# New written-out orders for two attention cores, two FFT convolutions and a front, with whole-tile and half-column forms of three PE steps

## The chip, the core and the metric

The kernel runs on one core of one Trainium2 chip, in one launch. The metric is the device time of an execution in microseconds (us), lower is better. The engines: TensorE (PE; its weight loads are listed as PEld), VectorE (DVE), ScalarE (ACT), GpSimd (POOL), and SyncE (SP), which here only issues DMAs.

## The reference

Two kinds of layers alternate, A, B, A, B, on a 2048 x 512 sequence in bf16. Both second layers use the same weights as the first ones.

```python
# A: dilated sliding-window attention, 32 heads of 16, window W=8, dilation 2
qkv = x @ wqkv                                   # (2048, 3*512)
idx = pos[:, None] - arange(8) * 2               # masked where negative
logits = einsum("bhsd,bhswd->bhsw", q, k[:, :, idx]) * 16**-0.5
attn = softmax(where(mask, logits, -1e9))
out = einsum("bhsw,bhswd->bhsd", attn, v[:, :, idx]) @ wo
# B: S4 layer, a causal convolution by FFT over 4096 points
K = einsum("dn,dnl,dn->dl", Cc, exp(dt*A*l), dt*Bc).real      # 512 x 2048
y = irfft(rfft(u, 4096) * rfft(K, 4096))[:2048] + u * Dskip
# the whole
x = x + A(layernorm(x)); x = x + B(layernorm(x))
x = x + A(layernorm(x)); x = x + B(layernorm(x))
```

## The kernel before, in words

The residual x_sb lies in SBUF with the sequence on 128 partitions x 16 rows (rows a = 0 to 15) and 512 features free. The execution has these stages, one after the other on the span of the profile: the filter K of layer B with the first front (layer norm, transposes, first projections), 0 to 110 us; the first attention core ("core 0"), 110 to 193; the first convolution ("conv 0") with the transform of the filter, 193 to 250; the second front, 250 to 275; "core 1", 275 to 365; "conv 1", 365 to 411; then the rest of the output's store.

**Who sets the order.** Nothing is scheduled: `tc.manual_schedule` keeps the instructions of DVE, ACT, PE and SP in the order of the program, and the program's order is written out in strings. CORE0 and CORE1 have one letter for each step of attention; ORDER0, ORDERF and ORDER1 have one token for each tile of the convolutions and the front. An engine takes its instructions in that order and waits at the first that isn't ready.

**A core** works on four blocks q of four rows. Letters: `q`, `v` project queries and values on PE (L215, L388) with a copy on ACT; `m` (mult, L332) multiplies queries with the eight shifted views of the keys on DVE into prod, two buffers; `l` (lsum, L340 to L344) sums each prod over the features of a head on PE into the logits L; `x` takes the maximum (mx, L404, DVE), `e`, `r`, `n` do exp, sums and normalisation (L416 to L438). A block below NCOL has its logits in columns (L340) and needs `T` (turn: transposes L444 on PE, a copy L446 on ACT); the others have them in rows (L344). `P` (pv_mult, L457, DVE) multiplies attention weights with eight shifted views of the values into pav, two buffers; `S` (pv_sum, L472, PE) transposes and sums pav in 64 half tiles of 64 partitions into po, copied by ACT to oT (L474); `O` (out_proj, L481, L483) projects and adds the residual. `a`, `b`, `d`, `t` are the layer norm of the result. In CORE0 the letters `A` to `H` copy eighths of the filter (k_part, L1379), turn about on ACT and DVE.

**A convolution** works on two halves g of the features. Tokens: `K`/`U` are f1 tiles of filter and signal (first FFT step, L769 on PE, evacuated from PSUM by evac, L758); `k`/`u` are f2 tiles (L776), u copied by ACT to ub (L835); `m` (u_mult, L819, L822) multiplies by the filter's transform on DVE; `y` (i1, L849) is the first inverse step, evacuated to z (L758); `z` (i2, L873 to L875) the second inverse step for four rows and one half g, which adds the residual, either on DVE while evacuating (L878) or by a matmul with the identity (L873) and a copy on ACT (L880). The letter at a token's end names the engine of the evacuation: A is ACT, D is DVE, B is half on each. In conv 1 the filter's transforms come from DRAM through a ring, kf_ring, whose loads SP issues. An i1 tile is 32 pairs of weight load and matmul on the two halves of the partitions:

```python
for tt, w, first in ((t1, C["Wp"], True), (t2, C["WpJ"], False)):
    for h in range(2):
        rows = slice(64 * h, 64 * h + 64)
        nc.tensor.matmul(p3[:, h, j, :], lhsT=tt[rows, dql, :], rhs=w[rows]..., start=first, stop=not first)
```

**The second front** (ORDERF) interleaves the last i2 tiles of conv 0 with layer norm (h, a, p, n), transposes (T) and the projections of keys and queries (P, E, Q) for core 1.

## Time and profile before

| what | value |
|---|---|
| runs | 413.06, 412.20, 412.77 us; median 412.77 |
| the profiled execution | 416.72 us; its span in the profile 414.9 us |
| instructions, bytes moved | 14876; 54.17 MB |
| mean granted clock of PE | 0.985 |
| DVE, L457 pav | 34 of 2.16 us on average, 72.9 us |
| DVE, L332 prod | 29 of 2.31 us, 66.3 us |
| ACT, L835 ub | 32 of 1.04 us, 32.1 us |
| PE, L472 po | 2048 matmuls, 35.9 us |

The span is the time from the first to the last instruction that the profiler recorded; what lies around it is 1.8 us here. A duration of a matmul in the profile is from its issue to its modelled end, and matmuls overlap, so the distance between the starts of two tiles tells more than their durations. "<-" names what ended a wait; "issue" is time in which nothing that the profile shows was waited for.

### The profile page before, as it was taken

What the parts mean: (1) busy time and instruction counts of PE and PEld (TensorE: products, weight loads), DVE (VectorE), ACT (ScalarE), POOL (GpSimd) and SP (SyncE); (2) the same over time, 40 slices, a digit from 0 to 9 for tenths busy, and PEclk for the clock granted to TensorE, in tenths of its full rate; (3) what the DMA queues carried; (4) which work ended last, traced back from release to release, by engine and by line L of the source; (5) the groups of instructions that cost most, each with busy time, mean ns of one, the idle gap of its engine ahead of it and who ended that gap; (6) DMA issues with size and microseconds to landing.
All of it is one profiled execution on the core that took longest, in us unless ns stands there. A gap on an engine that the chain in (4) does not pass through costs nothing.

```text
span 414.9 us, 14876 instructions
## 1 busy us (share of the span) xinstructions
PE 323.9 (78%) x6575; PEld 216.5 (52%) x6575; DVE 383.1 (92%) x500; ACT 327.9 (79%) x561; POOL 37.0 (9%) x48
## 2 busy tenths in 40 slices
PE   2000159899999977889997779999998889997785
PEld 2000126557533555656887668543445555576664
DVE  7999999999899999997998968979899999999965
ACT  5999999896456689997999988874666768889942
POOL 3000200000495000001300000000000020000000
PEclk9999999999999999999999999999999999999988
DMA  7930732122014845493244594830043046406406
GB/s 216 397 109 13 83 82 71 33 60 71 13 44 127 237 132 173 112 379 108 79 153 173 202 318 107 317 116 0 2 115 91 3 148 270 150 2 176 134 9 197
DMA packets 62322, 54.17 MB, mean 131 GB/s; under 512 B 33869, under 2 KB 50738, under 8 KB 60978
## 3 DMA queue, kind: packets, MB, share of 16 engines
q1 hardware_dynamic: 62250, 53.22, 41.7%
q8 instruction: 51, 0.84, 0.8%
q14 instruction: 13, 0.11, 0.1%
q10 hardware_dynamic: 8, 0.00, 0.0%
HBM read 30.15 MB, written 13.24 MB: 105 GB/s over the span
## 4 chain that ended last, share of the span: by engine, by line
PE 38%; DVE 20%; ACT 11%; issue 6%; DMA 6%; SPq 4%; DVEq 0%; ACTq 0%
PE pk L1195 5%; DVE prod L332 5%; PE pq L388 5%; DVE pav L457 4%; PE pp L1133 4%; DVE a1s L758 4%; PE po L472 3%; PE pq L483 3%; PE pp L272 3%; PE pq L215 3%; SPq L1300 2%; DMA w_sb<-w_dram 2%; PE L L340 2%; DMA kf_ring<-kf_dram 2%; DVE t L822 2%
## 5 line engine op out<-in xcount | busy, mean ns | idle before, releaser
L457 DVE TENSOR_TENSOR pav<-attn,v_ext 128x4096 bf16<-128x4096 bf16 (+1 forms) x34 | 72.9, 2155 | 0.4 <-PE pq L483 0.4
L332 DVE TENSOR_TENSOR prod<-qT,kT_ext 128x4096 bf16<-128x4096 bf16 x29 | 66.3, 2313 | 2.9 <-PE L L340 1.8
L472 PE MATMUL po<-ident,pav 64*128 64x64 bf16 x2048 | 35.9, 190 | 11.1 <-DVE pav L457 5.7
L472 PEld LDWEIGHTS <-pav 64*128 64x128 bf16 x2048 | 32.6, 95 | 22.1 <-DVE pav L457 12.3
L1123 PE MATMUL pt<-ident,x_blk 128*128 128x128 bf16 x64 | 6.3, 241 | 41.0 <-ACT x_blk L187 41.0
L1037 DVE TENSOR_TENSOR A_t<-A_t,pow_t 128x1024 bf16<-128x1024 bf16 (+4 forms) x46 | 38.1, 868 | 0.2
L776 PE MATMUL pb<-a1s,w_sb 128*128 128x64 bf16 x768 | 28.7, 196 | 6.9 <-ACT a1s L758 2.7
L483 PE MATMUL pq<-wop,oT 128*128 128x512 bf16 x128 | 33.7, 387 | 0.0
L835 ACT CAST ub<-pb 128x1024 bf16<-128x1024 f32 x32 | 32.1, 1038 | 1.8 <-ACT a1s L758 0.9
L388 PE MATMUL pq<-wv,xnT 128*128 128x512 bf16 x128 | 30.8, 380 | 0.3 <-ACT kgs L1203 0.3
L1133 PE MATMUL pp<-xnT,kT_ext 128*128 128x512 bf16 x96 | 26.2, 400 | 6.0 <-ACT qT L1138 3.1
L776 PEld LDWEIGHTS <-w_sb 128*128 128x128 bf16 x768 | 26.1, 100 | 9.3 <-issue 7.3
L758 DVE CAST a1s<-pb 128x1024 bf16<-128x1024 f32 x23 | 27.0, 1215 | 3.4 <-PE pb L769 3.4
L390 ACT CAST v_ext<-pq 128x512 bf16<-128x512 f32 x32 | 18.8, 587 | 14.3 <-PE pq L388 14.3
L1123 PEld LDWEIGHTS <-x_blk 128*128 128x128 bf16 x64 | 4.8, 108 | 43.4 <-ACT x_blk L187 42.0
L758 ACT CAST a1s<-pb 128x1024 bf16<-128x1024 f32 x25 | 24.9, 1036 | 2.2 <-PE pb L769 1.9
L474 ACT CAST oT<-po 128x512 bf16<-128x512 f32 x32 | 18.5, 578 | 8.1 <-PE po L472 7.8
L1195 PEld LDWEIGHTS <-A_t 128*64 128x64 bf16 (+1 forms) x512 | 21.8, 103 | 4.1 <-issue 0.6
L1195 PE MATMUL pk<-B_t,A_t 128*64 128x84 bf16 (+1 forms) x512 | 23.6, 201 | 0.0
L215 PE MATMUL pq<-xnT,kT_ext 128*128 128x512 bf16 x96 | 23.5, 379 | 0.0
L849 PEld LDWEIGHTS <-t 64*128 64x128 bf16 x1024 | 17.5, 97 | 11.4 <-issue 9.7
L849 PE MATMUL pb<-Wp,t 64*128 64x64 bf16 x512 | 19.5, 193 | 4.6 <-ACT ub L835 1.8
(240 smaller groups left out, 814.4 us busy)
## 6 DMA issues: line engine op xcount, KB each, us to landing
w_sb<-w_dram SPq DMA_DIRECT2D x8, 1024.0 KB, 7.1
w_dram<-xnT SPq DMA_DIRECT2D x1, 4096.0 KB
kf_ring<-kf_dram SPq DMA_DIRECT2D x13, 256.0 KB, 4.2
kf_ring<-kf_dram SPq DMA_DIRECT2D x26, 128.0 KB, 3.9
v_ext<-v_ext SPq DMA_DIRECT2D x4, 784.0 KB, 5.9
x_blk<-in_A_x_dram SPq DMA_DIRECT2D x4, 512.0 KB, 4.5
kT_ext<-in_A_wqkv_dram SPq DMA_DIRECT2D x4, 512.0 KB, 9.9
x_sb<-in_A_x_dram SPq DMA_DIRECT2D x4, 512.0 KB, 5.5
```

Source lines behind the costliest of these rows:

```text
L215: nc.tensor.matmul(pq[:], lhsT=self.wqk[:, dt, ft * P:(ft + 1) * P], rhs=self.xnT[:, dt, q * 512:(q + 1) * 512], start=(dt == 0), stop=(dt ...
L332: nc.vector.tensor_tensor(pr, self.qT[q][:, ft].unsqueeze(1).to_broadcast([P, W, 4, P]), kap, ALU.mult)
L388: nc.tensor.matmul(pp[:], lhsT=xnT[:, dt, a * P:(a + 1) * P], rhs=wv[:, dt, :], start=(dt == 0), stop=(dt == NDT - 1))
L457: nc.vector.tensor_tensor(pv[:, i], attn[:, n % 4].unsqueeze(2).to_broadcast([P, W, DH // parts, H]), vap, ALU.mult)
L472: nc.tensor.matmul(po[:, h, 0, i * nt + ft, :], lhsT=pvf[rows, i, w, ft * P:(ft + 1) * P], rhs=ident[rows, rows], start=(w == 0 and ft + i ...
L483: nc.tensor.matmul(pw[:], lhsT=oT[:, ftp, :], rhs=self.wo[:, ftp, :], start=False, stop=(ftp == NDT - 1))
L758: (self.nc.scalar.copy if eng == "act" else self.nc.vector.tensor_copy)(dst, src)
L776: nc.tensor.matmul(p2[:, j, :], lhsT=self.w2[:, ec * EC + j, :], rhs=a1s[:, ec * EC + j, :], start=True, stop=True)
L849: nc.tensor.matmul(p3[:, h, j, :], lhsT=tt[rows, dql, :], rhs=w[rows].rearrange("p m d -> p (m d)"), start=first, stop=not first)
L1037: return lambda: nc.vector.tensor_tensor(*args)
L1133: nc.tensor.matmul(pps[kind, b, ft][:], lhsT=la.wqk[:, dt, c:c + P], rhs=la.xnT[:, dt, b * 512:(b + 1) * 512], start=(dt == 0), stop=(dt = ...
L1195: nc.tensor.matmul(o, lhsT=lhs, rhs=Bt[:, ri, c * CH + ql].rearrange("p b g -> p (b g)"), start=(not half and j % 4 == 0 and ri == 0), sto ...
```

## The change

All of the order strings but the filter's (ORDERK) are new. Besides the order they change which engine evacuates which tile, and use new letters. `V` is a pv_sum that sums whole tiles of 128 partitions, 32 matmuls of 128 columns instead of 64 of 64 (one in core 0, five in core 1). `Y` is an i1 tile with whole weights, 16 matmuls of 128 columns instead of 32 of 64 (three in conv 0, two in conv 1); for it Wp and WpJ are stored once for each half of the partitions, with zeros in the other half. `w` and `v` are i2 tiles of half a g's columns, over eight rows with DVE's addition or over four rows with ACT's copy. In conv 1, w00, w01 stand for z00, z01, and v10, v11 for z10; z01 of conv 0 moves from ORDERF to the end of ORDER0. NCOL goes from 3 to 2 in both cores, so block 2's logits go into rows and its turn is gone. KROWS gives the last eighth of the filter's copy (`H`) to ACT instead of DVE. The unused tile "gap" of core 0 grows from 1024 to 1680 elements for each partition, and the tile of layer-norm statistics ln_bn is halved.

The number of PE matmuls goes from 6575 to 6513; DVE has two instructions fewer, ACT one copy more.

```diff
@@ -48,34 +48,35 @@
 zktkKkUEETkeUUktKTkkUkKTUUeKkkpkxpKUxkpUEUxUKkqUxUUUUpqoUkpoxKXUQxoUkpkKXZpxXxpxZZ
 """
 ORDER0 = """
-KD KA KA KD KA KA KD KA KD KA KD kA kA KD kA KD UA UD UA UD UA kD UA UD UA KD
-kA kD u kD kA u UA m KD m u u UD UA UA UA m UD u m KA UD u m u kA kD m kA UA
-kD u kA m kA kD u m u kA m m u u yD yA u m yA u m m m u u m m
+KD KD KA KA KA KD KA KA KD KA KD kA KD kA KD UA UA kD UA UA UD kA UD UA UA KD
+kA kD u kD kA u UA m KD u u m UA m UD UD UA UA u m KA u u m UD kA
+m u kD kA m kA kD kD UA kA u kA u m yA m u m yD yA u u m YA m m
+u u m m yA u m yA yA YD yD yA YD yA yA z01D yD yA
 """
 LATE0 = "a s t g r b m"
 ORDERF = """
-yA yA yA yA yA yA yD yA yA yA z01D yD yA yA z00A z10A z11A h01 h00 h10 a0 z12A
-p0 h11 z02A n0 a1 z03A h02 S T0 p1 E01D n1 E00A h12 a2 z13A P02 P01 h03 T1
-E10A Q00 E11D p2 P03 P00 n2 h13 P10 P12 a3 T2 E21D E20A p3 n3 P11 P13 P23 P21
-T3 E31D x1 E30A P20 P22
+yA z00A z10A h01 h00 h10 z11A a0 z12A h11 p0 S z02A n0 a1 z03A h02 p1 T0 E01D n1 h12 a2 E00A
+z13A P01 P02 T1 E11D E10A h03 Q00 p2 P00 n2 P03 h13 P10 P12 P11 T2 a3 E20A p3 E21D n3 P13 P23
+P20 P21 T3 E31D x1 E30A P22
 """
 ORDER1 = """
-UD UA UD UA UD UA UD UA UD UA UD u UD u u m UA u m UD UA m u m u m
-u m UA m u m u m u m u u yD yA u m yA m m u u u m yA m yA
-yA m yD yD yA yD yA yA yA yD z01D z03D yA yA z00D z02D z12D z11A z10D z13B
+UA UD UA UD UA UD UD UA UA UD UA u UD u u m u m m UA m u UD u m u
+UA m UA u u m m u m u m u yD m u yA yA m m u m u yA m u m
+yA yA yD YD yA YA yD z03D yD yA yA w000D yA yA w010D z02D v100A v110A z11A z12D z13B
 """
 
 CORE0 = """
-0mvvvvlmvvxlemqqlmqqlrmvvlnTmvvxlvemvlmvvlrmvvlnTqPxSePmqSOl1PrSO2Pm3qSOlPnT4SOPm56qSOl7P8ASOPmbBSO
-lPxdwCSeOPaaDSOPraaSOPnbSOPd9ESOPaaFGSOPaaHSOPbtStO
+vmvvv0lvmvqxleqqmlmvrlqmvvnTlmvvxlmevmlvvrlmvvlnTqPxSePS1qmOlPr4SO2PmqS3OlnP5SP67qmOSOlP8ASOPmPb
+BOSlCSwxdeOPaSaarPODVOPnbSOPd9SEOaaPaSOPGFaaPtOSHbSOt
 """
 CORE1 = """
-0m1l2ml3mqqlmqqvlmvvxlvemvvlmqqlrmqqvlnTmvvxlvemvvlmvvlrmvvlPnTqxSePmqSOlPrSOPmqSOlPnTSOPmqSOlPSO
-PmbSOlPxdwSeOPaaSOPraaSOPnbSOPdSOPaaSOPaaSOPbtStdaaaaO
+0m1l2ml3mvmqqqqlmlvmvvvxlqmvleqlrqmqlnTvmvvxlemvmvlvrvlmvvvlPnSTxqePSOmlqPrVOqOPmSPlnSOPOmqSlPVO
+PmbVOPlxdaVeOrPawSOPaaVOPnbSOPdSOPaSOPPaatSObStadaaaaO
 """
 ROWS0 = (0, 2, 1, 3, 4, 5, 6, 7, 8, 9, 10, 11, 12, 13, 14, 15)
 ROWS1 = (0, 2, 1, 3, 4, 5, 6, 7, 8, 9, 10, 11, 12, 13, 14, 15)
-NCOL = (3, 3)
+NCOL = (2, 2)
+KROWS = "ADADADAA"
 VROWS = (*range(0, 16, 2), *range(1, 16, 2))
 
 
@@ -366,7 +367,7 @@
                 self.load_wo(big)
             wk = c2.enter_context(tc.tile_pool(name=f"a{l}_wk", bufs=2, reuse_waits="tile"))
             if l == 0:
-                wk.tile([P, 1024], BF16, name="gap", bufs=1)
+                wk.tile([P, 1680], BF16, name="gap", bufs=1)
             self.prp = c2.enter_context(tc.tile_pool(name=f"a{l}_prod", bufs=2, reuse_waits="tile"))
             pavp = c2.enter_context(tc.tile_pool(name=f"a{l}_pav", bufs=2, reuse_waits="tile"))
             ps_q = c2.enter_context(tc.tile_pool(name=f"a{l}_ps_q", bufs=2, space=PSUM))
@@ -457,13 +458,23 @@
                     nc.vector.tensor_tensor(pv[:, i], attn[:, n % 4].unsqueeze(2).to_broadcast([P, W, DH // parts, H]), vap, ALU.mult)
                 pvs[n] = pv
 
-            def pv_sum(n):
+            def pv_sum(n, whole=False):
                 pv = pvs.pop(n)
                 parts = pv.shape[1]
                 pvf = pv[:].rearrange("p i w d h -> p i w (d h)")
                 po = ps_o.tile([P, 2, 2, NDT, 64], F32, name="po")
                 oT = wk.tile([P, NDT, P], BF16, name="oT")
                 nt = NDT // parts
+                if whole:
+                    pw = po[:, 0].rearrange("p b t q -> p (b t q)").rearrange("p (t q) -> p t q", t=NDT)
+                    for i in range(parts):
+                        for w in range(W):
+                            for ft in range(nt):
+                                nc.tensor.matmul(pw[:, i * nt + ft, :], lhsT=pvf[:, i, w, ft * P:(ft + 1) * P], rhs=ident[:],
+                                                 start=(w == 0 and ft + i == 0), stop=(w == W - 1), skip_group_check=True)
+                    nc.scalar.copy(oT[:], pw)
+                    oTs[n] = oT
+                    return
                 for i in range(parts):
                     for w in range(W):
                         for ft in range(nt):
@@ -533,17 +544,19 @@
                 m=calls(mult, *qft[nprod:]), l=calls(logit(lsum), *qft[nprod:]),
                 q=calls(q_proj, *qft[len(self.qT) * NDT:]), v=calls(v_proj, *((a,) for a in VROWS)),
                 x=calls(mx, *blocks), e=calls(sub_exp, *blocks), r=calls(recip, *blocks), n=calls(norm_p, *blocks), T=calls(turn, *blocks[:ncol]),
-                P=calls(pv_mult, *rows), S=calls(pv_sum, *rows), O=calls(out_proj, *rows[:15]), t=calls(x_stats, (12,), (13,)),
+                P=calls(pv_mult, *rows), O=calls(out_proj, *rows[:15]), t=calls(x_stats, (12,), (13,)),
                 b=calls(u_begin, (0, 4, "act", "pool"), (4, 8, "act", "act"), (8, 12, "act", "act")),
                 d=calls(u_end, (0,), (4,), (8,)),
                 a=calls(u_apply, *((a0, (a,)) for a0 in (0, 4) for a in range(a0, a0 + 4)), *((8, (a,), "act" if l and a < 10 else "dve") for a in range(8, 12))))
             ops = {key: iter(f) for key, f in ops.items()}
+            sums = iter(rows)
+            ops["S"], ops["V"] = (iter([lambda w=w: pv_sum(*next(sums), w)] * NA) for w in (False, True))
             for c in "".join(order.split()):
                 if c in ev:
                     ev[c]()
                 else:
                     next(ops[c])()
-            assert all(next(ops[c], None) is None for c in "mlqvxernPSOtb")
+            assert next(sums, None) is None and all(next(ops[c], None) is None for c in "mlqvxernPOtb")
             if l == 0:
                 out_proj(15)
                 return {"a": lambda: [u_end(8), u_apply(8, range(8, 12), "pool")], "s": lambda: x_stats(14), "t": lambda: x_stats(15),
@@ -662,9 +675,12 @@
             sine(ws[name][:], low16(wt[name][:].rearrange("p r a -> p (r a)")))
 
         def w_mask(name):
-            C[name] = cpool.tile([P, 32, 2], BF16, name=name)
-            nc.gpsimd.tensor_tensor(C[name][:], ws[name][:].unsqueeze(2).to_broadcast([P, 32, 2]),
-                                    dmask_m.unsqueeze(1).to_broadcast([P, 32, 2]), ALU.mult)
+            C[name] = cpool.tile([P, 2, 32, 2], BF16, name=name)
+            nc.gpsimd.memset(C[name][:], 0.0)
+            for h in range(2):
+                r = slice(64 * h, 64 * h + 64)
+                nc.gpsimd.tensor_tensor(C[name][r, h], ws[name][r].unsqueeze(2).to_broadcast([64, 32, 2]),
+                                        dmask_m[r].unsqueeze(1).to_broadcast([64, 32, 2]), ALU.mult)
 
         def w2_store():
             for s in range(4):
@@ -834,22 +850,25 @@
         ub = self.ub[g * NEC + ec] = self.wk.tile([P, DQG, EC], BF16, name="ub")
         nc.scalar.copy(ub[:], p2)
 
-    def i1(self, g, t, eng):
+    def i1(self, g, t, eng, whole=False):
         nc, C = self.nc, self.C
         if t == 0:
             self.S[g]["z"] = self.z0 if g == 0 else self.gpair("z", "t")[:, 0].rearrange("p (m c) -> p m c", m=2 * NA)
         z = self.S[g]["z"]
         t1, t2 = (self.S[g]["t"][:, i] for i in range(2))
-        p3 = self.ptile([P, 2, DQT, 64])
+        p3 = self.ptile([P, DQT, 2, 64] if whole else [P, 2, DQT, 64])
         for j in range(DQT):
             dql = t * DQT + j
             for tt, w, first in ((t1, C["Wp"], True), (t2, C["WpJ"], False)):
+                w = w[:].rearrange("p h m d -> p h (m d)")
+                if whole:
+                    nc.tensor.matmul(p3[:, j], lhsT=tt[:, dql, :], rhs=w, start=first, stop=not first)
+                    continue
                 for h in range(2):
                     rows = slice(64 * h, 64 * h + 64)
-                    nc.tensor.matmul(p3[:, h, j, :], lhsT=tt[rows, dql, :], rhs=w[rows].rearrange("p m d -> p (m d)"),
-                                     start=first, stop=not first)
+                    nc.tensor.matmul(p3[:, h, j, :], lhsT=tt[rows, dql, :], rhs=w[rows, h], start=first, stop=not first)
         self.evac(z[:, :, t * DQT * 4:(t + 1) * DQT * 4].rearrange("p m (j h d) -> p m j h d", h=2, d=2),
-                  p3[:].rearrange("p h j (m d) -> p m j h d", d=2), eng)
+                  p3[:].rearrange("p j h (m d) -> p m j h d" if whole else "p h j (m d) -> p m j h d", d=2), eng)
 
     def i2(self, g, t, eng):
 
@@ -878,6 +897,25 @@
             nc.vector.tensor_tensor(xr, p4[:], xr, ALU.add)
         else:
             nc.scalar.copy(x_sb[:, a0:a0 + n, dsl], p4[:])
+
+    def i2_cols(self, g, c, b, n, eng):
+
+        nc, x_sb, z = self.nc, self.x_sb, self.S[g]["z"]
+        w = DQG * 2
+        zs, a0 = slice(c * w, (c + 1) * w), b * n
+        xr = x_sb[:, a0:a0 + n, (2 * g + c) * w:(2 * g + c + 1) * w]
+        p4 = self.ptile([P, n, w])
+        add = eng == "dve"
+        for j in range(n):
+            a = a0 + j
+            if not add:
+                nc.tensor.matmul(p4[:, j, :], lhsT=self.ident[:], rhs=xr[:, j], start=True, stop=False)
+            nc.tensor.matmul(p4[:, j, :], lhsT=self.g2[:, 0, a, :], rhs=z[:, a, zs], start=add, stop=False)
+            nc.tensor.matmul(p4[:, j, :], lhsT=self.g2[:, 1, a, :], rhs=z[:, NA + a, zs], start=False, stop=True)
+        if add:
+            nc.vector.tensor_tensor(xr, p4[:], xr, ALU.add)
+        else:
+            nc.scalar.copy(xr, p4[:])
 
     def run(self, order, u, done=lambda g, t: None, k=None, late=(), more={}):
         late, cnt = list(late), self.cnt
@@ -895,6 +933,15 @@
                 self.i2(*ix, eng)
                 done(*ix)
                 continue
+            if op in "wv":
+                rows = 8 if op == "w" else 4
+                self.i2_cols(*ix, rows, eng)
+                for b in range(ix[2] * rows // 4, (ix[2] + 1) * rows // 4):
+                    half = cnt["w", ix[0], b] = cnt.get(("w", ix[0], b), 0) + 1
+                    if half == 2:
+                        done(ix[0], b)
+                continue
+            op = "y" if op == "Y" else op
             n = cnt[op] = cnt.get(op, -1) + 1
             g, t = divmod(n, 8)
             if op in src:
@@ -912,7 +959,7 @@
             elif op == "m":
                 self.u_mult(g, t)
             else:
-                self.i1(g, t, eng)
+                self.i1(g, t, eng, tok[0] == "Y")
 
     def swap_psum(self):
         self.c_ps.close()
@@ -1375,7 +1422,7 @@
         nc.vector.tensor_tensor(kr[0:1, 0, :], kr[0:1, 0, :], dsk[:, h * 256:(h + 1) * 256], ALU.add)
 
     def k_part(h, j):
-        cp = nc.scalar.copy if j % 2 == 0 else nc.vector.tensor_copy
+        cp = nc.scalar.copy if KROWS[h * 4 + j] == "A" else nc.vector.tensor_copy
         cp(kp[:, h * 64 + j * 16:h * 64 + (j + 1) * 16, :, :],
            krs[h][:, :, j * 64:(j + 1) * 64].rearrange("p a (q r) -> p q a r", r=4))
 
```

More of the change, by code (lines that the diff above doesn't have):

```diff
@@ L1336 @@
     lnst = dict(s1=cpool.tile([P, NA], F32, name="ln_s1"), s2=cpool.tile([P, NA], F32, name="ln_s2"),
-                bn=cpool.tile([P, NA, 2, 6], F32, name="ln_bn"), junk=cpool.tile([P, D], BF16, name="ln_junk"),
+                bn=cpool.tile([P, NA, 1, 6], F32, name="ln_bn"), junk=cpool.tile([P, D], BF16, name="ln_junk"),
                 mh=cpool.tile([P, 4], F32, name="ln_mh"))
```

## The prediction

> **What bounds the kernel now.** I read the page first, then the table by stage, then the chain that ended last, VectorE's (DVE's) own timeline, and the waits.
>
> The page's totals, and its row for the queue that brings instructions:
>
> ```profile
> PE 323.9 (78%) x6575; PEld 216.5 (52%) x6575; DVE 383.1 (92%) x500; ACT 327.9 (79%) x561; POOL 37.0 (9%) x48
> q8 instruction: 51, 0.84, 0.8%
> ```
>
> DVE is the bound on average, but a share of 92% leaves 31.8 us of the 414.9 in which it waits. TensorE (PE) has 6575 matmuls and as many weight loads, 13,150 instructions; 51 packets of instructions is one per 258 of them. In the packets' own rows each holds 16 KB, 256 instructions of 64 bytes, and almost all are PE's.
>
> The table by stage (columns: length, then busy time of PE, PEld, DVE, ACT, POOL; granted clock, DMA share, GB/s):
>
> ```profile
> 110.00:193.00 83.00, 73.17 (x1482) 41.17 (x1483) 78.19 (x61) 62.53 (x126) 20.82 (x17) 1.00 0.51 156
> 193.00:238.00 45.00, 39.16 (x1216) 35.16 (x1215) 43.10 (x58) 42.71 (x48) 6.05 (x8) 1.00 0.43 155
> 238.00:252.00 14.00, 10.92 (x360) 9.14 (x360) 8.92 (x16) 12.24 (x14) 0.35 (x1) 1.00 0.88 287
> 252.00:275.00 23.00, 22.90 (x180) 14.77 (x179) 19.75 (x69) 18.34 (x33) 0.00 (x0) 1.00 0.65 218
> 275.00:364.00 89.00, 83.47 (x1536) 44.96 (x1534) 85.22 (x71) 60.84 (x130) 2.89 (x1) 0.98 0.27 91
> 364.00:415.00 51.00, 38.20 (x1098) 33.35 (x1096) 41.62 (x40) 35.88 (x40) 0.00 (x0) 0.91 0.36 105
> ```
>
> These are core 0 (attention), convolution 0 up to its last u tile, its end, the second front, core 1, convolution 1 with the store. The cores are DVE's; convolution 0 is shared by DVE and ACT to within an evacuation; the front is PE's (22.90 of 23); the two ends of the convolutions belong to nobody, and there the time is to be had.
>
> The chain in the last 20 us, from where the last u_mult (L819) has ended:
>
> ```profile
> 394.86 0.39 issue
> 395.25 1.22 DVE xnT L758
> 396.51 0.38 PE pb L849 x14
> 396.89 1.46 issue
> 398.35 1.93 PE pb L849 x82
> ```
>
> PE stops in the middle of an i1 tile (L849), 14 matmuls into it, for 1.46 us, waiting for nothing that the profile shows. Counted in program order, that instruction is the first of a block of 256. The others fall on boundaries too: 390.35, 394.35, 398.35 are three in a row, 4.0 us apart, and 247.34 (a stop of 1.10 in the chain) is one in convolution 0. The fetch rows show why 4.0: a packet starts 1.5 to 1.7 us after PE has entered a block (392.05, 395.95) and the next block is entered 2.3 to 2.4 us after that. So a block that PE could run in less than 4.0 us still takes 4.0. A block of half-tile i1 is four tiles of 0.47 us (starts of L849 tiles, 394.61, 395.07, 395.54): 1.9 us of work. Its effect on DVE:
>
> ```profile
> 396.38 1.21 DVE L758 CAST z<-pb 128x1024 bf16<-128x1024 f32 x1
> 400.32 1.23 DVE L758 CAST z<-pb 128x1024 bf16<-128x1024 f32 x1 [2.74 <-PE pb L849]
> 402.14 2.35 DVE L878 TENSOR_TENSOR x_sb<-pb,x_sb 128x1024 bf16<-128x1024 f32 x2 [0.59 <-PE pb L875]
> ```
>
> After the gaps the clock halves: i2 matmuls are 0.21 us apart from 400.2 to 402.2 and 0.11 after that.
>
> Core 0's waits on DVE:
>
> ```profile
> DVE a1s L758 <- PE pb L769: 2.4, 1, 2.4
> DVE prod L332 <- PE L L340: 1.8, 1, 1.8
> DVE mx L404 <- PE L L322: 0.8, 1, 0.8
> ```
>
> **Basis.** The profiled execution took 416.72 us (span 414.9 and 1.8 around it), 3.95 above the median of the runs, 412.77. Differences are worked out on its rows and taken from the median unscaled (1% of 7 us is nothing). A change under 0.2%, 0.8 us, can't be told from none.
>
> **The change part by part.**
>
> *Convolution 1, up to the last u_mult.* One f1 tile goes from DVE to ACT: DVE has seven of 1.13 us back to back (8.01 for 7 at 365.76) where it had eight, and its u_mults follow without a gap in both. DVE is solid from 365.76 to 397.6, so −1.1. ACT gains 0.92 there and has slack (its idle in the tail alone is 8 us); two u tiles come so close to their mults that 0.3 may be lost. Filter loads (kf_ring, SP's queue) move with the mults that free their slots. Taken: −0.9.
>
> *Convolution 1, the end.* Call T0 the end of the last mult, 394.11 less a fraction in before; DVE's last operation ends at 410.96, T0+16.85. After: two of the sixteen i1 tiles are whole (16 matmuls of 128 columns, 32 instructions instead of 64). No row has that form; by streaming, 16×128 columns against 8×256 of an i2 tile (L874/875, 8×0.11) is 0.88 us. w000D, w010D are 16 matmuls of 128 columns, 0.88 as well; v100A, v110A 12 of them, 0.66; instead of three i2 tiles of 0.88. So PE gets 0.82 more to do, and 2×32 instructions less in i1. Laid on the new program order with the same offset: the block that straddles T0 holds 3 half tiles and 2 whole (3.2 us), the next 3.6 half tiles, z03 and 5 matmuls of w000 (2.85), the one behind it 5.2 us, the last 2.75. The straddling one is entered about T0−1.6 (last u copy ends T0−1.2, the f2 tile before it about T0−2.3, then 1.4 i1 tiles). By the rule of 4.0 the others are entered at T0+2.4, T0+6.4 and, unstopped, T0+11.6; PE ends at T0+14.4, the last evacuation of half a tile (0.59) at T0+15.0. DVE has 10.9 us of work there, which fits. Gain 1.85. If the clock halves again for 2 us, 1 us of it goes; if the blocks cost nothing, 1.7 more comes. Bounds 0 and −3.5; taken −1.9.
>
> The Trainium skill, "Runtime: NRT & Kernel Launch", section "Instruction fetch mechanics", says that the sequencer fetches the next 16 KiB (256 instructions) while it executes the current ones, and that crossing costs little, "mostly hidden". By that rule the stops above aren't the blocks', and the sum for this part would be about 0. The trace agrees on the 256 and not on the hiding: 1.46 us of stop at 396.89.
>
> *Convolution 0.* Evacuations: ACT one fewer in all (y 13→11, U 10→11; 0.95), DVE one more (1.13). ACT is the bound up to 249.85, where the front's first copy stands: 53.3 busy of 56.3, and 1.28 of its idle time is the stop at 247.34. But the order also moves work: in front of the last u, ACT has three more evacuations and DVE one fewer, which fills ACT's 2.3 us of idle time and delays the last u by 1 to 2.5. Behind it, ACT has 7 i1 tiles instead of 11 and PE 720 instructions instead of 912 (three whole tiles, two of them here). In blocks: the last f2 stands just ahead of a boundary, the next two blocks (2.5 and 3.3 us of work) take 4.0 each, then 2.1 tiles: the front's first tile begins 9.2 us behind the last f2, in before 13.05 (235.28 to 248.33). So −3.85 and +1 to +2.5: −1.35 to −2.85, and −2.2 by ACT's account (0.95+1.28). Taken −2.1. At 287 GB/s the block before 247.34 took 4.8 us instead of 4.0, so bounds 0 and −4. Three half-tile pairs becoming whole cost PE 1.2, behind evacuations.
>
> *Second front.* The same seven ACT-form i2 tiles of 12×0.109 us, transposes and projections; z01D moved ahead of it. PE-bound before and after: 0 (±0.5); it passes on what convolution 0 wins.
>
> *Core 0.* k_part H moves from DVE (0.41, L1379) to ACT (1.03); ACT loses one attn copy after turn (1.01, L446), since the third block's logits now go into rows. So ACT is even, DVE −0.4. Turn's 8 transposes (0.46) go, lsum gets 0.25 to 0.4 longer, four times (row form 0.80 to 0.95, column form 0.55): PE +0.9, hidden behind 78.19 us of DVE. mx of the last block stands later behind mults: its 0.8 goes, and if the logits come late it returns as up to 1.8 (the prod wait). At the handover one f1 tile of the filter stands ahead of row 15's pv_sum on PE; DVE's first a1s can start at once and the second waits as in before: 1.0 of the 2.42. The copy of H may delay oT by 0.5. Sum −0.4−0.8−1.0+0.3 = −1.9; bounds +1 and −3.
>
> *Core 1.* Same row form; five pv_sums whole: 32 matmuls of 128 columns at 55 ns, 1.77 us (turn's 8 of 128 columns in 0.46 give 57 ns; the i2 rows halved, 55) against 1.04 for 64 half ones: +3.65 in all. PE becomes 88.0 busy of 89, so its cover is thin. DVE's own waits in core 1 add to 3.7 us (1.2 before ex, 1.0 before prods), of which the order may save some. Taken −0.5; bounds −2 and +4.5 (all the added PE time).
>
> *Others.* Four small POOL operations instead of two and two memsets, in the beginning where POOL has 42 us idle; the larger gap moves addresses: 0.
>
> Sum: −0.9 −1.9 −2.1 −1.9 −0.5 = −7.3: 412.77−7.3 = 405.5.
>
> **The rivals.**
>
> 1. *The stops aren't the blocks'.* Then they stay where fast i1 stands, and the forms only add PE time. Left: core 0 −1.9, core 1 −0.5, ACT's saving −0.95, the f1 tile −0.9, against +0.8 in the end: −3.45, 409.3. For it: two i1 stops of convolution 0's boundaries (238.65, 242.52) are short, since ACT paces PE there. Against: the regular 4.0. It is what the Trainium skill's rule above would leave of the change.
> 2. *Core 1 turns to PE.* pav has two buffers, so a pv_sum that ends late holds DVE's next but one pav. "PEld po" waits for pav reach 1.7 us; if each whole pv_sum costs DVE 1.7 and the row form 1.3, core 1 gets 5×1.7+1.3 = 9.8 longer; with the other −6.8: +3, 415.8. It decides from 7.6 us of new DVE waits in core 1. For it: PE is never idle from 275 to 311 and would be 88 of 89. Against: the trace's pv_sums wait for DVE (12.3 us), not DVE for them (0.4).
> 3. *Won and given back.* With core 1 at +4.5 and convolution 0 at its bound 0, −0.9−1.9−1.9+4.5 = −0.2: 412.6.
>
> **How the numbers follow.** Forecast 0.57 (own range 401.5 to 408.5), rival 1 0.15, rival 2 0.18, rival 3 0.07, and 0.03 for lower than all. Rivals 2 and 3 spread over no change: faster 0.71, same 0.06, slower 0.23. The range takes in the forecast's bounds, rivals 1 and 3 and a part of 2: 401 to 414.5, which leaves some 0.06 below and 0.12 above.
>
> **What would show it.** Right: DVE's 2.74 before a z tile gone from convolution 1, boundaries there still 4.0 us apart but with less stop, the last DVE operation about T0+15; first front copy 4 us earlier (core 0 and convolution 0 together); DVE's 2.4 before a1s at about 1.4; core 1 at 88 to 89 us with PE near 88. Wrong: new rows "DVE pav ← PE po" or "prod ← PE L" of several us in core 1; i1 stops as long as before; a whole tile over 0.9 us.

## The result and the profile after

The changed kernel takes 411.67 us (median of 20 runs, 410.82 to 413.12), the kernel before 413.23 (20 runs, 411.36 to 416.16): a ratio of 0.996, 95% interval 0.9945 to 0.9975, or 1.6 us less (1.0 to 2.3). The forecast was 7.3 less. The profiled execution of the changed kernel took 412.14 us with a span of 410.3, so it is 0.5 above its median. That of before, on which the forecast was summed, was 3.5 above the median that 20 runs gave: a comparison of the two traces alone says −4.6, three times what the runs say.

The page of the changed kernel, its busy times and its instruction queue:

```profile
PE 322.0 (78%) x6467; PEld 227.0 (55%) x6513; DVE 384.2 (94%) x498; ACT 326.7 (80%) x562; POOL 46.0 (11%) x52
q8 instruction: 51, 0.84, 0.9%
```

As many packets of instructions as before. POOL, with four more instructions, is busy 9.0 us longer; this comes back below.

The table by stage of the changed kernel, columns as before:

```profile
110.00:193.00 83.00, 73.73 (x1576) 45.75 (x1592) 80.91 (x62) 62.97 (x126) 27.54 (x17) 1.00 0.54 163
193.00:238.00 45.00, 39.29 (x1201) 35.46 (x1195) 42.91 (x59) 44.74 (x51) 6.03 (x8) 1.00 0.41 148
238.00:252.00 14.00, 12.39 (x307) 10.74 (x306) 12.23 (x26) 10.36 (x11) 0.35 (x1) 1.00 0.97 305
275.00:364.00 89.00, 83.43 (x1487) 51.91 (x1503) 83.63 (x71) 59.79 (x129) 2.89 (x1) 1.00 0.28 90
364.00:410.00 46.00, 35.22 (x1052) 31.55 (x1046) 38.30 (x34) 35.72 (x40) 0.00 (x0) 0.97 0.39 117
```

ACT is full up to the last u (44.74 of 45), and DVE is busier behind it (12.23 of 14 us, before 8.92), as the order asked for; core 1's PE did not grow to 88. POOL's 20.82 in core 0 became 27.54.

DVE's waits in core 0 and its handover (the three that the prediction shows stood there before):

```profile
DVE a1s L774 <- PE pb L785: 1.6, 1, 1.6
DVE k_perm L1426 <- DMA k_rl<-kd_dram: 0.2, 1, 0.2
```

DVE's timeline at the end of conv 1 (start, duration, what; idle time before it in brackets):

```profile
393.68 1.23 DVE L774 CAST z<-pb 128x1024 bf16<-128x1024 f32 x1
...
399.37 1.23 DVE L916 TENSOR_TENSOR x_sb<-pb,x_sb 128x1024 bf16<-128x1024 f32 x1 [0.88 <-PE pb L914]
400.51 1.22 DVE L897 TENSOR_TENSOR x_sb<-pb,x_sb 128x1024 bf16<-128x1024 f32 x1
403.76 1.82 DVE L897 TENSOR_TENSOR x_sb<-pb,x_sb 128x1024 bf16<-128x1024 f32 x2 [2.04 <-PE pb L894]
```

The wait of 2.74 before a z tile is gone; the last mult ends at 391.4 and DVE at 405.6, T0+14.2 (forecast T0+15.0). This looked like a gain of 2.5 us, and isn't one, as the first experiment shows.

### The profile page after: what moved, and what is told of

It reads as the page before. It is cut to its first block, busy times and chain, and to the rows that moved or that the text cites. A ratio compares the mean times of both kernels' runs of the same rounds, so it can differ in the third digit from the quotient of the medians.

```text
span 410.3 us, 14708 instructions
## 1 busy us (share of the span) xinstructions
PE 322.0 (78%) x6467; PEld 227.0 (55%) x6513; DVE 384.2 (94%) x498; ACT 326.7 (80%) x562; POOL 46.0 (11%) x52
## 4 chain that ended last, share of the span: by engine, by line
PE 35%; ACT 18%; DVE 17%; issue 7%; DMA 3%; SPq 2%; DVEq 0%; ACTq 0%
PE pk L1242 5%; DVE pav L458 5%; PE pq L389 5%; DVE prod L333 4%; ACT a1s L774 4%; PE pp L1180 4%; ACT ub L851 3%; PE pp L273 3%; PE pq L216 3%; PE pq L494 2%; DVE t L835 2%; PE pb L869 2%; PE po L483 2%; PE L L341 2%; DMA v_ext<-v_ext 1%
## 5 line engine op out<-in xcount | busy, mean ns | idle before, releaser
L483 PEld LDWEIGHTS <-pav 64*128 64x128 bf16 x1664 | 26.2, 95 | 15.1 <-DVE pav L458 8.5
L483 PE MATMUL po<-ident,pav 64*128 64x64 bf16 x1664 | 29.0, 190 | 6.6 <-DVE pav L458 3.9
L494 PE MATMUL pq<-wop,oT 128*128 128x512 bf16 x122 | 31.6, 379 | 2.5 <-issue 1.9
L1180 PE MATMUL pp<-xnT,kT_ext 128*128 128x512 bf16 x87 | 25.0, 405 | 7.0 <-ACT qT L1185 2.9
L792 PEld LDWEIGHTS <-w_sb 128*128 128x128 bf16 x768 | 25.0, 98 | 8.0 <-issue 5.2
L774 DVE CAST a1s<-pb 128x1024 bf16<-128x1024 f32 x21 | 25.0, 1217 | 4.1 <-PE pb L785 4.1
L774 ACT CAST a1s<-pb 128x1024 bf16<-128x1024 f32 x27 | 26.4, 1052 | 2.3 <-PE pb L785 2.2
L494 PEld LDWEIGHTS <-oT 128*128 128x128 bf16 x128 | 12.4, 98 | 14.0 <-ACT oT L485 1.1
L485 ACT CAST oT<-po 128x512 bf16<-128x512 f32 x26 | 15.0, 577 | 6.0 <-PE po L483 5.9
L389 PEld LDWEIGHTS <-xnT 128*128 128x128 bf16 x128 | 11.6, 97 | 14.1 <-issue 1.9
```

The lines of the kernel that those rows point to most:

```text
L389: nc.tensor.matmul(pp[:], lhsT=xnT[:, dt, a * P:(a + 1) * P], rhs=wv[:, dt, :], start=(dt == 0), stop=(dt == NDT - 1))
L483: nc.tensor.matmul(po[:, h, 0, i * nt + ft, :], lhsT=pvf[rows, i, w, ft * P:(ft + 1) * P], rhs=ident[rows, rows], start=(w == 0 and ft + i ...
L494: nc.tensor.matmul(pw[:], lhsT=oT[:, ftp, :], rhs=self.wo[:, ftp, :], start=False, stop=(ftp == NDT - 1))
L774: (self.nc.scalar.copy if eng == "act" else self.nc.vector.tensor_copy)(dst, src)
L792: nc.tensor.matmul(p2[:, j, :], lhsT=self.w2[:, ec * EC + j, :], rhs=a1s[:, ec * EC + j, :], start=True, stop=True)
L1180: nc.tensor.matmul(pps[kind, b, ft][:], lhsT=la.wqk[:, dt, c:c + P], rhs=la.xnT[:, dt, b * 512:(b + 1) * 512], start=(dt == 0), stop=(dt = ...
```

## The experiments

Ratios are against the kernel before in runs on the same chip; its median was 413.2 to 413.9 us there. Eight to twelve executions of each kernel (seven in one case) give intervals of ±0.2 to 0.4%, about 1 us, so the traces are read beside them. A "boundary" is the place of a PE instruction whose number in the program, shifted by a constant found on the first trace, is a multiple of 256; a stop is the time from the start of the weight load before it to its own start, which is 0.1 to 0.2 us more than the idle time that the chain lists as "issue".

### 1. Is the trace of before a typical one?

No edit: the kernel before, profiled once more.

> The kernel before, unchanged, for a second profiled execution. The first one took 416.72 us where the median of its runs is 413.23, and the forecast was summed on its rows. Theory T (the profiled execution was not typical): this one takes 412.5 to 414, the two tail waits of DVE on i1 in conv 1 (2.74 before a z tile, 0.59 before the first x_sb) are smaller by about 2 to 3 us together, and its tail from the end of the last u_mult is about 14 us instead of 16.85. Rival S (the time lies elsewhere): the tail is 16.5 to 17 us again and the difference stands in other stages. Time against before: same.

Measured: 413.66 us, ratio 0.9999 (0.9981 to 1.0018), the profiled execution 413.63. Its DVE at the end of conv 1:

```profile
395.98 1.22 DVE L758 CAST z<-pb 128x1024 bf16<-128x1024 f32 x1
398.25 1.23 DVE L758 CAST z<-pb 128x1024 bf16<-128x1024 f32 x1 [1.05 <-PE pb L849]
```

Where the first trace had 2.74 us, 1.05 stand here, and the tail from the last mult to DVE's end is 14.07 us instead of 16.77. The boundaries stand at the same instructions, but 3.73, 3.45 and 3.58 us apart, with stops of 0.75, 0.55 and 0.00 where the first trace had 1.33, 1.67 and 0.00, and the granted clock is 1.00 from 385 to the end. Theory T holds. With this trace the difference of the spans, 411.8 to 410.3, is −1.5: close to that of the medians.

The three stops of the second trace (0.76 at 389.66, then 0.75 and 0.55) hardly cost anything either. In the profiled execution of before with the larger gap (experiment 4), whose PE instructions are the same, these boundaries are 3.83, 3.66 and 3.80 us apart with no stop over 0.02. PE's i1 tiles wait 3.1 us there for evacuations, ACT's copies of u and a mult (1.2 in the second trace), DVE still waits before its z tile, and the tail is 13.76 us, 0.3 shorter:

```profile
398.74 1.23 DVE L758 CAST z<-pb 128x1024 bf16<-128x1024 f32 x1 [0.73 <-PE pb L849]
```

So a stop that goes is in large part replaced by another wait. Its last mult also ends 0.8 us later than in the second trace, so this is a comparison and no test.

### 2. Do the places of the boundaries matter?

Padding that nothing reads, in PE's idle time at 9 us, moves every later boundary (64 matmuls are 128 instructions, half a block; 128 are a whole one):

```diff
+        pad = pst.tile([P, 4, P], F32, name="pt")
+        for _ in range(64):
+            nc.tensor.matmul(pad[:, 0, :], lhsT=ident[:], rhs=ident[:], start=True, stop=True)
```

> The kernel before with 64 further matmuls (128 PE instructions) at 9 us, where PE is idle until 48 us; nothing reads them. Every later block boundary of 256 instructions falls 128 instructions earlier in the program. Theory F (a block takes at least 4.0 us): stops move to other tiles, boundaries in conv 1's i1 stay about 4.0 us apart, and the time changes by up to 1 us either way. Rival (stops belong to the code where they stood, not to the boundaries): stops stay at the same matmuls, the time is the same within 0.3 us.

> The changed kernel with the same 128 PE instructions in front. If its orders owe their gain to where the blocks fall, that is lost: 1 to 2 us slower than the changed kernel (411.67), so at the time of before (ratio 0.999 to 1.002). If the gain is from evacuations and order alone: ratio 0.995 to 0.997, as the changed kernel.

> The changed kernel with 128 matmuls that nothing reads (256 PE instructions, one whole block) in PE's idle time at 9 us. It is the control for the run with 64 of them: the boundaries fall at the same instructions as in the changed kernel. Theory F (position of the boundaries): as the changed kernel, ratio 0.995 to 0.997, stop at the end of conv 0 under 1 us. Rival (the padding itself costs): 1.002 or more.

Measured: before with 64: 417.72 us, 1.0087 (1.0054 to 1.012), where at most 1 us was expected; its boundaries in conv 1 are 4.36, 3.71 and 3.20 us apart, not 4.0. After with 64: 414.59, 1.0006 (0.998 to 1.0032), about 2 us over the changed kernel's 0.996. After with 128: 411.58, 0.9957 (0.9935 to 0.9979), as the changed kernel. So it is the place of the boundaries, not the padding: half a block costs, a whole block costs nothing. Where it costs is seen in the chain of after with 64, at the end of conv 0:

```profile
243.98 1.08 PE pb L869 x73
245.06 2.81 issue
247.87 0.24 PE pb L869 x5
```

One stop of 2.81 us (3.03 from load to load) five matmuls before the end of the last i1 tile; in the changed kernel the same stage has one of 0.70. In the next 5 us the granted clock is 0.73 (first figure behind the busy times):

```profile
250.00:255.00 5.00, 5.00 (x36) 3.97 (x35) 3.10 (x13) 2.74 (x3) 0.00 (x0) 0.73 0.78 201
```

and the front's i2 matmuls are 0.21 us apart from 249.5 to 252.7. Core 1's first prod comes 3.9 us later (276.2 against 272.3). Before with 64 has two such stops, 1.85 and 2.15.

### 3. The parts of the change, one put back at a time

conv 1's order of before in the changed kernel (`ORDER1` alone):

> The changed kernel with the order of conv 1 (ORDER1) from before, so without its whole i1 tiles and half-column i2 tiles; cores, conv 0 and front stay new. Forecast's terms: conv 1 was to bring 2.8 us, and the trace of the changed kernel shows its tail 2.55 shorter than the first trace of before. If that is what runs show too, this one takes 414.2 us (ratio 1.002). By theory T (a typical tail of before is already short), 411.7 to 412.7 (ratio 0.996 to 0.999).

Measured: 411.51 us, 0.9949 (0.9925 to 0.9974): not slower than the changed kernel. conv 1's new order is worth nothing in the runs.

The cores of before:

> The changed kernel with both cores as before (CORE0, CORE1, NCOL 3, H's copy on DVE); convolutions and front stay new. The forecast gave the cores 2.4 us: 414.1 (ratio 1.002). The traces show core 0 and its handover 3.1 us earlier at the second a1s, of which 1.5 already at its first prod, and core 1 0.2 to 0.5 shorter: by them 414.5 to 415 (ratio 1.002 to 1.004). Rival (conv 0's order holds the gain): 411.5 to 412.5, ratio 0.996 to 0.998.

Measured: 415.79, 1.0052 (1.0024 to 1.0081), with a stop of 2.46 us at the end of conv 0, since the old cores have another number of PE instructions. So once more with 57 matmuls of padding, which put the boundaries back:

> The changed kernel with the cores of before and 57 matmuls of padding (114 PE instructions), so that conv 0 and the second front have their boundaries where the changed kernel has them. The run with old cores and no padding was 1.0052, with a stop of 2.46 us at the end of conv 0. Theory F: the stop is back under 1 us, core 1's first prod 2.5 to 4 us earlier than in that run, and what is left is the cores' own price, 1.5 to 3 us: ratio 0.999 to 1.003. Rival (the old cores' own order costs the 4 us): ratio 1.004 to 1.006.

Measured: 413.96, 1.001 (0.9989 to 1.0031), the stop 0.38. In the profiled executions core 1 starts 4.4 us earlier than without padding (273.9 against 278.3). The cores' own worth is about 0.005, 2 us; the other 1.8 of the first run's loss was where the boundaries fell.

conv 0 and the second front of before (`ORDER0`, `ORDERF`), without and with 80 matmuls of padding:

> The changed kernel with conv 0 and the second front in the order of before (ORDER0, ORDERF), so without three whole i1 tiles. The forecast gave conv 0 2.1 us: 413.8 (ratio 1.001). The traces show 0.5 us lost between core 0's handover and the first prod of core 1, not won: 411 to 411.7 (ratio 0.995 to 0.9965), but the block boundaries fall elsewhere, and a long stop at the end of conv 0 may add 1 to 3 us (ratio up to 1.004).

> The changed kernel with conv 0 and second front in the order of before, and 80 matmuls of padding (160 PE instructions), so that the boundaries at the end of conv 0 and in conv 1 fall as in the changed kernel. Without padding this was 0.9984 (412.76 us), with a stop of 1.55 us. Theory F: the new order of conv 0 and front brings nothing of its own; 0.995 to 0.997, as the changed kernel, and core 1's first prod at 272 to 273. Rival (the order itself, with its three whole tiles, brings the 1 us): 0.998 or more. By the forecast (2.1 us): 1.001.

Measured: 412.76, 0.9984 (0.9961 to 1.0008), and with padding 412.01, 0.9977 (0.9949 to 1.0006). The two ratios don't differ, but in the traces core 1's first prod moves from 273.7 to 272.26, where the changed kernel has it (272.30). By trace, conv 0's new order brings nothing once the boundaries are the same; the runs give it 0.7 us, less than their interval.

Whole i1 tiles as half tiles (`Y` as `y`), and whole pv_sums as half ones (`V` as `S`, with 96 matmuls of padding for conv 0's sake):

> The changed kernel with the five whole i1 tiles as half tiles (Y as y in the same places): 0.41 us less of streaming for each, 32 more PE instructions for each, so a block boundary more than half a block earlier in conv 0's end. Forecast's rule (blocks shorter than their fetch wait for it): 1 to 2 us slower than the changed kernel at the end of conv 0, ratio 0.998 to 1.001. Rival (evacuations set the pace, the form doesn't matter): ratio 0.995 to 0.997.

> The changed kernel with the six whole pv_sums as half tiles (V as S in the same places) and 96 matmuls of padding (192 instructions), which with the 64 of core 0's half tiles make one whole block: conv 0 has its boundaries as in the changed kernel, conv 1 is 64 instructions off. The forecast gave whole pv_sums no gain of their own and up to 0.7 us of loss each in PE time, hidden by DVE: same as the changed kernel or up to 0.5 faster, ratio 0.9945 to 0.997. Rival (fewer PE instructions in core 1 save fetch stops there): 1 us slower, 0.998 or more.

Measured: half i1 413.66, 1.0004 (0.9983 to 1.0025), about 1.8 us slower: stops of 1.33 and 0.67 at the end of conv 0, of 1.14, 1.14, 0.39 and 0.73 in conv 1. The whole tile, which takes PE 0.89 us (16 starts 55 to 56 ns apart) against 0.47, is the better one here; how much of that is its fewer instructions and how much the boundaries' other places, this run doesn't tell apart. Half pv_sums 412.39, 0.9969 (0.9943 to 0.9995): the changed kernel's 0.996 lies in its interval. In the traces core 1 takes 84.8 us instead of 83.9 from its first prod to its last pav; its stops are 0.5 at most, as with whole ones, so it isn't the fetches. DVE waits 1.1 longer for DMAs before its pavs there (2.3 against 1.2). Why, no run tells.

### 4. The gap

Only the unused tile's size, in the kernel before and back in the changed one:

```diff
-                wk.tile([P, 1024], BF16, name="gap", bufs=1)
+                wk.tile([P, 1680], BF16, name="gap", bufs=1)
```

> The kernel before with nothing changed but the size of the unused tile of core 0, 1024 to 1680 elements. All runs with the larger tile have core 0's first prod at 111.2 us, all with the smaller at 112.7 to 112.9, where DVE waits 1.8 us for a PE lsum, and the run with the old cores has 111.2 too. Theory G (prod's first buffer lay on memory that an earlier lsum still read): first prod at 111.2, the wait gone, and 1 to 1.5 us of it at the end: ratio 0.9965 to 0.998. The forecast put this at 0 us: ratio 1.000.

> The changed kernel with the unused tile back at 1024 elements. Core 0's first prod is expected at 112.7 to 112.9 again, 1.6 us later. Theory P (POOL takes the time back: its four passes between 110 and 137 then meet more or fewer of DVE's mults, 2.28 us alone and 2.69 beside POOL): the last pav of core 0 ends 0.3 to 1.0 later than in the changed kernel (188.15), ratio 0.996 to 0.9985. Rival (the whole 1.6 us goes through, since no wait for PE follows in the new order): 189.8, ratio 0.9985 to 1.001.

Measured: before with the large gap 413.12, 0.9984 (0.9961 to 1.0006). Core 0's first prod is at 111.06 instead of 112.70, as theory G has it, but core 0's last pav ends at 189.60, where the first trace of before has 189.61 and the second 190.39. Where most of it went, in POOL's timelines, of before and then of before with the large gap:

```profile
110.69 1.48 POOL L698 TENSOR_SCALAR g_i<-g_i,aux 128x512 int32<-128x512 int32 x2
...
113.20 5.15 POOL L698 TENSOR_SCALAR g_i<-g_i,aux 128x512 int32<-128x512 int32 x2
```

```profile
110.81 5.53 POOL L698 TENSOR_SCALAR g_i<-g_i,aux 128x512 int32<-128x512 int32 x2
```

The same two POOL instructions take 1.48 us while DVE waits and 5.53 while DVE multiplies, and DVE's multiplications beside them take longer too (two prods 4.80 us instead of 4.49):

```profile
111.06 4.80 DVE L332 TENSOR_TENSOR prod<-qT,kT_ext 128x4096 bf16<-128x4096 bf16 x2
```

What is left behind these passes, 0.5 us against the first trace of before and 0.7 against the second, meets a wait of the last mx (L404) for PE. That wait differs between executions: mx starts at 169.40 with the large gap and in the first trace of before, at 170.18 in the second. The second trace, then the large gap:

```profile
170.18 1.23 DVE L404 TENSOR_REDUCE mx<-L 128x128 bf16<-128x1024 f32 x1 [1.14 <-PE L L322]
```

```profile
169.40 1.22 DVE L404 TENSOR_REDUCE mx<-L 128x128 bf16<-128x1024 f32 x1 [1.12 <-PE L L322]
```

So the first trace alone would say that the gap's 1.6 us are all lost, and that isn't so: in the three traces of the old cores with the small gap the last pav ends at 189.61, 190.39 and 190.79, in the three with the large gap at 189.36, 189.60 and 189.70, 0.7 earlier on average. In the changed kernel's order, which has no such wait, the small gap takes 413.02, 0.9985 (0.9962 to 1.0009), and core 0's last pav ends at 189.54 instead of 188.15; 0.76 of these 1.39 us are another wait, of a pav on a DMA, which leaves 0.6. In either order, then, some 0.6 to 0.7 us of the 1.6 are kept in the traces; the runs say 0.7 and 1.0, within intervals of the same size.

### 5. Why stops are long or short

```diff
+        def traffic():
+            for i in range(2):
+                nc.sync.dma_start(junk[i], A_wqkv)
-        fb.run(ORDER1, u, store)
+        fb.run(ORDER1, u, store, more={"X": traffic})
```

with the token X behind ORDER1's last m; junk is a new tile in DRAM.

> The changed kernel with 3 MB copied from one place in DRAM to another (nothing reads it) during the end of conv 1, where the DMA engines are otherwise almost idle; SP issues it right behind its last filter load, at about 385 us. The block boundaries stand where they stood (388.4, 393.1, 396.4 us, stops of 0.02, 0 and 0.06 us). Theory D (instruction fetches wait behind bulk transfers, which is why the longest stops stand at the end of conv 0, beside 300 to 380 GB/s): fetches there start 2 to 4 us after the boundary before them instead of 1.0 to 1.5, and stops of 1 to 3 us appear at two of the boundaries. Rival (the fetch has its own way): stops as before; only the output's stores come later.

Measured: 416.72 us, 1.0058 (1.0021 to 1.0095). The chain at the second boundary:

```profile
394.69 0.28 PE pb L869 x12
394.97 2.08 issue
397.05 0.47 PE pb L869 x20
```

The 5 us before it, of the changed kernel and then of this one (the last two figures are DMA share and GB/s):

```profile
390.00:395.00 5.00, 4.58 (x128) 3.94 (x129) 4.95 (x6) 3.86 (x5) 0.00 (x0) 1.00 0.02 3
```

```profile
390.00:395.00 5.00, 4.13 (x140) 3.56 (x136) 5.00 (x5) 4.75 (x6) 0.00 (x0) 1.00 1.03 406
```

The fetch for this block started 4.54 us after the boundary before it (394.57 after 390.03), while the copy was still running (DMA share 1.30 from 394 to 395, 0.50 from 395 to 396); in the changed kernel 1.44 (389.84 after 388.40), and the block came without a stop. Theory D holds, at one boundary instead of the two expected (at the other 0.38): beside bulk transfers the instruction fetch starts later. Behind the last mult this trace is 2.4 us longer than that of the changed kernel; of the other 1.6 us, 1.5 were lost in core 0, ahead of the copy, and this experiment doesn't explain them. At the end of conv 0, where 320 to 350 GB/s move from 240 to 245 us, the same boundary of the same program had stops of 1.30 and 0.39 in the two traces of before, and 2.77 in the one with the larger gap, whose instructions are the same ones.

### 6. The output, and a faster version

conv 1's half-column i2 tiles as whole rows, and the same with z10 on DVE:

```diff
-yA yA yD YD yA YA yD z03D yD yA yA w000D yA yA w010D z02D v100A v110A z11A z12D z13B
+yA yA yD YD yA YA yD z03D yD yA yA z00D yA yA z01D z02D z10A z11A z12D z13B
```

> The changed kernel with the half-column i2 tiles of conv 1 put back to whole rows (w000D, w010D as z00D, z01D; v100A, v110A as z10A in the same places). Theory O (output): a block of rows is stored only when both of its halves are done, so in the changed kernel no store is issued from 396.1 to 400.6 and seven of eight come after; the last one lands 4.7 us before the span's end instead of 3.5 to 3.9. With whole rows the stores spread out again: 0.7 to 1.2 us faster than the changed kernel, ratio 0.993 to 0.9945. Rival (the stores don't matter, the half tiles' earlier evacuations do): ratio 0.996 to 0.998.

> The version with whole rows in conv 1's i2 (0.9931, 410.88 us) with z10 evacuated by DVE's addition instead of ACT's copy: 4 matmuls of 0.11 us less on PE, which sets the pace there, 1.1 us more on DVE, which waits 2.9 us there. 0.3 to 0.5 us faster: ratio 0.992. Rival (DVE becomes the last): same or 0.7 slower, 0.993 to 0.995.

Measured: 410.88 us, 0.9931 (0.9905 to 0.9957), and with z10 on DVE 410.28, 0.992 (0.9893 to 0.9946). DVE ends at the same 405.6 us in both as in the changed kernel; it is the stores behind it that got shorter. SP in the changed kernel (one store at 396.1, then seven), and the time that the stores take to land in the changed kernel and with whole rows:

```profile
400.62 5.40 SPq L1514 DMA_DIRECT2D out_dram<-x_sb  x7
```

```profile
DMA to landing us min/median/max: 3.3/4.0/4.2
```

```profile
DMA to landing us min/median/max: 2.2/2.2/4.1
```

A store of four rows needs both of its half columns, so w000 and w010 hold the second of the eight stores back from 398.50 to 400.62 and the third from 400.61 to 401.06. From DVE's end to the span's end it is 4.76 us instead of 3.55. That these 1.2 us are the price of the half columns isn't shown, though. Four other runs of experiments 2 and 3 (padding of 64, old conv 0 without padding, half i1, half pv_sums) have the half columns and the same pattern, one store and then seven, and end 3.72 to 3.73 behind DVE; the other traces with half columns have 4.20 to 4.76, the three of the changed kernel with whole rows 3.55 to 3.56, and those of before, with whole rows too, 3.97 to 4.26. So theory O is right on the order of the stores and at least 0.2 us of its price; what makes the stores land later in some executions is open. The runs' 0.003 agrees with theory O but is no wider than its interval.

The version with z10 on DVE is the fastest that was run. In its trace the tail is 0.4 us shorter than with z10 on ACT (13.73 against 14.17), as expected, but its last mult ends 0.4 later; whether z10 adds anything lies within the interval.

## Why the prediction was wrong

Faster was right; the size was not (−7.3 against −1.6). Three terms of the sum failed: the end of conv 1 (−1.9), conv 0 (−2.1) and core 1 (−0.5) brought nothing or cost time in the traces. Step by step, with the second trace of before (411.8 us span) against that of the changed kernel (410.3), all in us:

| step | forecast | traces | by runs |
|---|---|---|---|
| up to core 0's first prod (the gap) | 0 | −1.8 | gap: −0.7 in the old order, −1.0 in the new |
| core 0 up to the second a1s | −1.9 | −2.1 | both cores −2 |
| conv 0 and front | −2.1 | +1.5 | −0.7 |
| core 1 to conv 1's first a1s | −0.5 | +0.7 | |
| conv 1 to the last mult | −0.9 | −0.8 | conv 1 as a whole +0.5 |
| its end, to DVE's last | −1.9 | +0.1 | |
| stores | not priced | +0.8 | half columns +1.2, cause in part open |
| sum | −7.3 | −1.5 | −1.6 |

The rows are rounded. Each figure by runs carries an interval of about 1 us either way, and they aren't parts of one sum.

- **The basis.** "Differences are worked out on its rows and taken from the median unscaled." A stop of 1.46 us and its neighbours were costed as if every execution had them. They were most of what put that execution over its median: the forecast took out of 412.77 what was only in 416.72. That failed for the end of conv 1: the absolute forecast (T0+15.0) was near the measured T0+14.2, but the second trace of before ends at T0+14.1 too, so the gain was nil.
- **The rule of 4.0 us.** The place of the stops was right, and so was their cause, the blocks, against rival 1: a shift by half a block costs 2 to 3.6 us, one by a whole block nothing. The Trainium skill, "Runtime: NRT & Kernel Launch", section "Instruction fetch mechanics", has such crossings "mostly hidden"; here they aren't. The number was wrong. The equal distances belonged to that execution, which itself has a pair 3.87 us apart with a stop of 0.23 (238.65 to 242.52): other pairs with a stop at their end lie 3.2 to 3.7 us apart where other DMAs are quiet, and 3.8 to 7.0 beside bulk DMA (7.02 with the copy). And a block that isn't stopped isn't shorter by the stop: without stops PE's blocks in conv 1 took 3.7 to 3.8 us (experiment 1).
- **conv 0.** This term was summed from two sizes, and both were off. Behind the last f2 tile the forecast had 9.2 us to the front's first tile instead of 13.05, −3.85. From that tile's first matmul it is 13.65 in the first trace of before, 13.03 in the second and 11.31 after, −1.7 on the second: blocks took 4.9 and 4.4 us there instead of 4.0 (boundaries at 235.25, 240.12, 244.50). And the work moved ahead of the last u cost about 3.2 of what core 0 had won instead of 1 to 2.5, with ACT at 44.74 of 45: the second a1s stands 3.85 earlier than in the second trace, that f2 tile only 0.6. Together that is the +1.5 of the table.
- **Core 0.** The sum was near, by other terms: the mx wait's 0.8 went as said, and the handover's gain was larger (the second a1s stands 4.2 us behind the last pav instead of 5.8 in the second trace, 1.6 where 1.0 was taken). The gap, costed at 0, mattered, less by far than the 1.8 us at the first prod (experiment 4).
- **Core 1.** Rival 2's added PE time was hidden: a whole pv_sum takes 1.74 us from its first matmul to its last against 0.92 of a half one, but PE is busy 83.43 of 89 (83.47 in the first trace of before, 80.84 in the second), and DVE has no new wait of size on a pv_sum. DVE's other waits, of which the order was to save some, are as long as before (3.6 us against 3.3 in the second trace), and from the first prod to the last pav it is 0.3 less. But a1s of conv 1 starts later (7.6 us behind the last pav instead of 6.6). With conv 1's old order it is 7.1, so about half of that is the new order's, whose first f1 tile goes to ACT; the rest is open.
- **Output.** The half columns were priced in PE time, and the DMAs that wait for both halves weren't looked at. How much of the +0.8 is theirs is open (experiment 6).

Of the signs that were set, DVE's wait before the z tile went and its wait before a1s came out at 1.6 (forecast 1.4), but the boundaries in conv 1 are 4.75, 3.24 and 5.43 us apart instead of 4.0, and the first front copy is 2.3 us earlier than in the second trace of before instead of 4.

## What to carry to other kernels

Before pricing a wait, take a second profile of the same program: a wait that is random in size belongs to the execution, and subtracting it from a median counts a gain that isn't there. On a PE with many small matmuls, count instructions as well as time where DMA is busy, and check a reordering with a padded version, since a change of a few instructions far ahead moves the stops. When an output tile is cut across the pieces that a store takes, the store waits for the last piece, here one store of eight by 2.1 us.

## What the runs showed of the hardware

- A block of 256 PE instructions is fetched by one packet of 0.9 to 1.8 us, and where PE waits for it (stops of 0.5 us and more), it is entered 2.2 to 2.9 us after that fetch starts. The fetch of such a block starts 1.0 to 1.7 us after the boundary before it in quiet stretches, and up to 4.5 beside 400 GB/s of other traffic.
- Behind stops of 3.03 us (changed kernel with 64 matmuls of padding) and 2.46 (with the old cores) the granted clock was 0.5 for 3.4 us, and matmuls lay 0.21 us apart instead of 0.11; behind stops of 2.77 (before with the large gap) and 2.27 (with the copy) it stayed at 1.00. Stops of 0.76, 0.75 and 0.55 us in a row left it at 1.00 too, those of 1.16, 1.33 and 1.67 in the first trace of before did not. So the length of a stop alone doesn't tell whether the clock falls.
- POOL's integer tensor_scalars take 0.74 us each beside an idle DVE and 2.6 to 3.9 in passes that DVE's bf16 multiplications cover; of these some take 2.6 to 2.7 us instead of 2.28.
